# Decode attention with a gated FFN: wo in seven pieces, sixteen partitions of its first piece by way of GpSimd

## The chip, the cores and the metric

The kernel runs on one core of a Trainium2 chip. The metric is the device time of one launch in microseconds, here as the median of several runs. Beside the timed runs there is one execution recorded by the hardware profiler; all times inside the kernel come from that one and count from the start of its span.

## The reference

One token of width 576 goes through a layer norm, and then through two branches whose outputs are added to it: attention of 32 heads over a cache of 16,384 keys and values of width 128, and a feed-forward block with a gelu gate.

```python
xn = _layernorm(x)                                   # (1, 1, 576)
q = (xn @ wq).reshape(B, Sq, 32, 128)                # wq: 576 x 4096
scores = einsum("bhqd,bhkd->bhqk", q, k_cache) * 128 ** -0.5
o = einsum("bhqk,bhkd->bhqd", softmax(scores), v_cache)
A = o.reshape(B, Sq, 4096) @ wo                      # wo: 4096 x 576
g, u = xn @ w_gate, xn @ w_up                        # 576 x 4608 each
Bout = (gelu(g) * u) @ w_down                        # w_down: 4608 x 576
return x + A + Bout
```

Everything is fp32. The two caches are 537 MB, the weights some 50 MB; every byte is read once.

## The kernel before

The program is written in a tile framework that inserts the waits between engines. All large loads are issued by SyncE (SP, the helper `load`, L67 and L68) into three large slots of 64 KB a partition: one of tag "v" (`vslot`) and two of tag "k" (`kslot`). A load may be issued when the slot's last reader is done. First come wq, w_gate and w_up, whose products TensorE makes (`project`, L132). Then the loop over heads (L238) runs: K of head h goes into a kslot; VectorE multiplies it by the query (L204) and sums it over the head's width (L205); TensorE, ScalarE and VectorE make the softmax (L207 to L218); V of the head before goes through TensorE (`pv`, L225). Every fourth head `out_heads` takes the sums out of PSUM (L230 to L235).

Behind the last head stands the part that the change touches. Three tiles are taken: `ta` (a vslot), `tb` (the kslot of the last K) and `te` (the kslot that holds the last V). A matrix of many rows is laid out with several rows to a partition: w_down has 36 of 576 columns on each of the 128 partitions, wo has 32. Such a stretch of 576 columns on all partitions is called a row here; its product takes one column of `hT` or `oT` as the stationary operand. `load_rows` (L276) loads n rows with one transfer:

```python
def load_rows(t, at, src, lo, n):
    load(t[:, at * D : (at + n) * D], src[:, lo * D : (lo + n) * D])
    return [t[:, (at + j) * D : (at + j + 1) * D] for j in range(n)]
```

w_down comes in pieces of 28 rows (into `ta`) and 8 (into `tb`), wo in pieces of 20 (into `tb`, behind w_down's 8) and 6, 3, 2, 1 (into `te`, so not before `pv` of the last head is done). SP issues them in this order. The attention's output is normalised, transposed and written to `oT` by a small transfer from GpSimd (L299); two more from GpSimd (L307) bring x into `x2`.

`add_out` (L267) does the products on TensorE, at L270. For w_down and the first 26 rows of wo a row is split in two halves of 288 columns; even rows go to `acc`, odd ones to `PO[0]`. The last `WO_Q` = 6 rows are split in four quarters of 144 columns, into four partitions of `acc4`. In front of the third row from the end VectorE adds the two half-width sums to x (L314, L315), and TensorE adds the result into the quarters (L318). After the last row VectorE copies `acc4` to SBUF (L322) and SP stores it (L323). Each fp32 matmul appears as two matmul records in the trace.

Of the kernel before, what the change touches and what calls it, by code (L numbers as in the profile page):

```python
# [8 lines left out]
F32 = mybir.dt.float32  # L9
# [4 lines left out]
P = 128  # L14
H, SK, DH = 32, 16384, 128
D, DF = 576, 4608
# [11 lines left out]
WD_T = DF // P  # L28
WO_T = HD // P
WD_PIECES = (28, 8)  # L30
WO_PIECES = (20, 6, 3, 2, 1)
WO_A = 20
WO_Q = 6
QUART = D // 4
HG = 4
PW = 4 * HG
# [4 lines left out]
def kernel(ctx: ExitStack, tc: tile.TileContext, x, k_cache, v_cache, wq, wo, wg, wu, wd, out):  # L41
    nc = tc.nc
    cpool = ctx.enter_context(tc.tile_pool(name="cpool", bufs=1))
# [10 lines left out]
    xf = x.rearrange("b s d -> (b s) d")  # L54
# [3 lines left out]
    wov = wo.rearrange("(p t) f -> p (t f)", t=WO_T)  # L58
# [8 lines left out]
    def load(dst, src):  # L67
        nc.sync.dma_start(dst, src)  # L68
        return dst
# [5 lines left out]
    row3, tails, at = {}, {}, 0  # L75
# [191 lines left out]
    def add_out(groups, lhs, w, last=False):  # L267
        n = D // len(groups)
        for i, g in enumerate(groups):
            nc.tensor.matmul(g, lhs, w[:, i * n : (i + 1) * n], start=id(g) not in seen, stop=last)  # L270
            seen.add(id(g))

    half = [[pairs[i][32 * (2 * i + j) : 32 * (2 * i + j) + 1, :HALF] for j in range(2)] for i in range(2)]
    quart = [acc4[32 * g : 32 * g + 1, :] for g in range(4)]

    def load_rows(t, at, src, lo, n):  # L276
        load(t[:, at * D : (at + n) * D], src[:, lo * D : (lo + n) * D])
        return [t[:, (at + j) * D : (at + j + 1) * D] for j in range(n)]

    ta, tb, te = vslot(), kslot(), kslot()  # L280
    a, b = WD_PIECES
    wd_rows = load_rows(ta, 0, wdv, 0, a) + load_rows(tb, 0, wdv, a, b)
    wo_rows, lo = [], 0
    for n in WO_PIECES:
        wo_rows += load_rows(tb, b + lo, wov, lo, n) if lo < WO_A else load_rows(te, lo - WO_A, wov, lo, n)
        lo += n
# [22 lines left out]
    for j, w in enumerate(wo_rows):  # L309
        if j < WO_T - WO_Q:  # L310
            add_out(half[j % 2], oT[:, j : j + 1], w, last=j >= WO_T - WO_Q - 2)
            continue
        if j == WO_T - 3:
            nc.vector.tensor_add(x2[:64], x2[:64], PO[0][64:, :HALF])  # L314
            nc.vector.tensor_add(x2[:64], x2[:64], acc[:64, :HALF])  # L315
            for i, g in enumerate(quart):
                r, lo = 32 * (i // 2), i % 2 * QUART
                nc.tensor.matmul(g, ones[r : r + 1, :1], x2[r : r + 1, lo : lo + QUART], start=False, stop=False)  # L318
        add_out(quart, oT[:, j : j + 1], w, last=j == WO_T - 1)
# [32 lines left out]
```

## Time and profile before

| | us |
|---|---|
| median of 3 runs | 1372.63 (1372.15 to 1372.82) |
| the profiled execution's own time | 1372.94 |
| its span | 1371.1 |
| VectorE busy | 1128.3 (82% of the span) |
| TensorE busy | 403.5 (29%) |
| ScalarE, GpSimd busy | 38.9, 6.3 |

The page lists busy times, queues, the chain of work that ended last and the costliest groups. In a row of the chain stand start, length and what ran or was waited for; in a row of the timeline the bracket gives the idle time before an instruction and what ended it; in a row of DMA issues the last number is the time from issue to landing. The DMA share of a window is the mean busy share of the core's sixteen DMA engines. PEclk is the clock granted to TensorE, 1.00 being full speed.

### The profile page before, as it was taken

What the parts mean: (1) busy time and instruction counts of PE and PEld (TensorE: products, weight loads), DVE (VectorE), ACT (ScalarE), POOL (GpSimd) and SP (SyncE); (2) the same over time, 40 slices, a digit from 0 to 9 for tenths busy, and PEclk for the clock granted to TensorE, in tenths of its full rate; (3) what the DMA queues carried; (4) which work ended last, traced back from release to release, by engine and by line L of the source; (5) the groups of instructions that cost most, each with busy time, mean ns of one, the idle gap of its engine ahead of it and who ended that gap; (6) DMA issues with size and microseconds to landing.
All of it is one profiled execution on the core that took longest, in us unless ns stands there. A gap on an engine that the chain in (4) does not pass through costs nothing.

```text
span 1371.1 us, 6374 instructions
## 1 busy us (share of the span) xinstructions
PE 403.5 (29%) x2861; PEld 117.2 (9%) x2861; DVE 1128.3 (82%) x160; ACT 38.9 (3%) x128; POOL 6.3 (0%) x17
## 2 busy tenths in 40 slices
PE   4421232322321232322212332322212232322146
PEld 1110000100000000100000000100000000100012
DVE  1059999889888888899888888898888888998830
ACT  0000000000000000000000000000000000000000
POOL 0010000000000000000000000000000000000000
PEclk9775566566556656665556556556556656566577
DMA  9999999999999999999999999999999999999997
GB/s 403 439 428 444 433 428 427 436 434 438 430 430 433 436 435 434 429 432 434 434 433 434 433 434 434 428 434 434 438 432 429 428 436 434 442 427 429 428 427 303
DMA packets 11908, 588.05 MB, mean 429 GB/s; under 512 B 1621, under 2 KB 1641, under 8 KB 2026
## 3 DMA queue, kind: packets, MB, share of 16 engines
q1 hardware_dynamic: 11528, 587.60, 99.2%
q8 instruction: 22, 0.36, 0.1%
q0 software_dynamic: 352, 0.06, 0.0%
q14 instruction: 4, 0.03, 0.0%
q10 hardware_dynamic: 2, 0.00, 0.0%
HBM read 587.60 MB, written 0.00 MB: 429 GB/s over the span
## 4 chain that ended last, share of the span: by engine, by line
DMA 50%; DVE 45%; PE 3%; another core or an unknown queue 1%; issue 1%; ACT 0%; SPq 0%; DVEq 0%
DMA kslot<-in_A_k_cache_dram 45%; DVE kslot L204 23%; DVE s L205 22%; DMA kslot<-in_A_wo_dram 3%; DMA kslot<-in_A_wq_dram 2%; PE pg L132 2%; PE acc L270 1%; PE pt L211 0%; DVE pm L209 0%; PE pq L147 0%; ACT qrow L139 0%; DVE nm L213 0%; DVE kslot L314 0%; DVE kslot L315 0%
## 5 line engine op out<-in xcount | busy, mean ns | idle before, releaser
L204 DVE TENSOR_TENSOR kslot<-kslot,qs 128x16384 f32<-128x16384 f32 (+1 forms) x33 | 551.3, 16706 | 90.6 <-DMA kslot<-in_A_k_cache_dram 90.6
L205 DVE TENSOR_REDUCE s<-kslot 128x128 f32<-128x16384 f32 (+1 forms) x33 | 551.2, 16703 | 3.3
L225 PE MATMUL po<-vslot,pe 128*16 128x512 f32 x1984 | 283.6, 736 | 645.6 <-DMA vslot<-in_A_v_cache_dram 630.2
L225 PEld LDWEIGHTS po<-vslot,pe 128*16 128x16 f32 x1984 | 66.9, 113 | 846.8 <-issue 829.9
L211 PE MATMUL pt<-ident,pm 128*1 128x128 f32 x32 | 11.9, 372 | 237.6 <-DVE pm L209 237.6
L265 DVE MEMSET acc<- 128x144 f32 x1 | 0.2, 178 | 74.3 <-ACT vslot L166 74.3
L132 PE MATMUL pg<-kslot,xnb 128*32 128x384 f32 (+1 forms) x208 | 24.2, 629 | 33.5 <-DMA kslot<-in_B_w_gate_dram 18.4
L314 DVE TENSOR_TENSOR kslot<-kslot,po 64x288 f32<-64x288 f32 x1 | 0.5, 455 | 36.1 <-PE po L270 36.1
L217 ACT ACTIVATE nb<-pb 128x1 f32<-128x1 f32 x32 | 5.5, 171 | 811.8 <-PE pb L215 811.8
L211 PEld LDWEIGHTS pt<-ident,pm 128*1 128x1 f32 x32 | 2.5, 79 | 261.0 <-DVE pm L209 220.2
L215 PE MATMUL pb<-nm,ones 1*128 1x1 f32 x64 | 18.2, 351 | 13.1 <-DVE nm L213 13.1
L213 DVE TENSOR_REDUCE nm<-pt 1x1 f32<-1x128 f32 x32 | 8.9, 278 | 14.9 <-PE pt L211 14.9
L215 PEld LDWEIGHTS pb<-nm,ones 1*128 1x128 f32 x64 | 15.9, 306 | 22.1 <-DVE nm L213 12.0
L147 PE MATMUL pq<-qrow,ones 1*128 1x512 f32 x16 | 15.6, 1072 | 0.0
L270 PE MATMUL acc<-kslot,oT 128*1 128x288 f32 (+1 forms) x100 | 10.8, 410 | 8.2 <-DMA kslot<-in_A_wo_dram 8.2
L218 ACT ACTIVATE pe<-s,nb 128x128 f32<-128x128 f32 x32 | 12.8, 402 | 1.0
L132 PEld LDWEIGHTS pg<-kslot,xnb 128*32 128x32 f32 x208 | 7.2, 129 | 51.4 <-DMA kslot<-in_B_w_gate_dram 19.2
L291 DVE RECIPROCAL rl<-pl 128x32 f32<-128x32 f32 x1 | 0.4, 358 | 13.7 <-PE pl L289 13.7
L270 PE MATMUL acc<-vslot,hT 128*1 128x288 f32 x56 | 8.9, 488 | 7.8 <-DMA vslot<-in_B_w_down_dram 7.8
L230 ACT ACTIVATE o<-po 128x512 f32<-128x512 f32 x8 | 4.8, 597 | 221.8 <-PE po L225 221.8
L234 PE MATMUL pc<-sel,o 128*128 128x4 f32 x64 | 8.4, 255 | 5.7 <-ACT o L230 5.7
L209 DVE TENSOR_REDUCE pm<-s 128x1 f32<-128x128 f32 x32 | 9.2, 286 | 1.1
(74 smaller groups left out, 112.9 us busy)
## 6 DMA issues: line engine op xcount, KB each, us to landing
kslot<-in_A_k_cache_dram SPq DMA_DIRECT2D x2, 4096.0 KB, 27.1
vslot<-in_B_w_down_dram SPq DMA_DIRECT2D x1, 8064.0 KB, 29.0
kslot<-in_B_w_gate_dram SPq DMA_DIRECT2D x1, 6912.0 KB, 55.6
kslot<-in_B_w_up_dram SPq DMA_DIRECT2D x1, 6912.0 KB
kslot<-in_A_wo_dram SPq DMA_DIRECT2D x1, 5760.0 KB, 42.1
vslot<-in_B_w_gate_dram SPq DMA_DIRECT2D x1, 2304.0 KB, 29.0
vslot<-in_B_w_up_dram SPq DMA_DIRECT2D x1, 2304.0 KB, 37.5
kslot<-in_B_w_down_dram SPq DMA_DIRECT2D x1, 2304.0 KB, 28.8
```

The lines of the kernel that those rows point to most:

```text
L132: nc.tensor.matmul(pg[32 * q : 32 * q + 32, b, :size], lhs, rhs[:, lo : lo + size], start=k == 0, stop=k == len(steps) - 1)
L147: nc.tensor.matmul(pq, ones[r : r + 1, :], qrow[r : r + 1, lo : lo + QH * DH], start=True, stop=True)
L204: tc.keep_in_program_order(nc.vector.tensor_mul(blk, blk, Q[h].to_broadcast([P, n, DH])))
L205: nc.vector.tensor_reduce(S[h][:, i : i + n], blk, axis=AX.X, op=ALU.add)
L209: tc.keep_in_program_order(nc.vector.reduce_max(pm, S[h], axis=AX.X))
L211: nc.tensor.transpose(pt[:1, :P], pm, ident)
L213: tc.keep_in_program_order(nc.vector.tensor_reduce(nm, pt[:1, :P], axis=AX.X, op=ALU.max, negate=True))
L215: nc.tensor.matmul(pb[:, :1], ones[:1, :], nm, start=True, stop=True)
L218: nc.scalar.activation(pe4, S.pop(h).rearrange("p (k s) -> p k s", s=4), AF.Exp, bias=nb, scale=SCALE, accum_out=lsum[:, h : h + 1])
L225: nc.tensor.matmul(PO[h // HG % 2][q : q + PW, :], pe[:, lo : lo + PW], vt[:, k * 512 : (k + 1) * 512], start=i == 0 and k < 4, stop=i == ...
L234: nc.tensor.matmul(pc[:, :HG], o4[:, j * DH : (j + 1) * DH], pick[:, j, :], start=j == 0, stop=j == 3)
L270: nc.tensor.matmul(g, lhs, w[:, i * n : (i + 1) * n], start=id(g) not in seen, stop=last)
```

## The change

wo comes in seven pieces, 14, 8, 5, 2, 1, 1, 1, instead of five. The first (14 rows) goes into `tb`, the others into `te`. Quarter width now holds for the last ten rows, and the addition of x stands in front of the fifth row from the end.

The 14 rows are loaded by SP on partitions 0 to 111 alone. Partitions 112 to 119 and 120 to 127 come by one GpSimd transfer each, and in front of each of these stands a tiny GpSimd transfer of eight partitions of 288 B, from x into a tile `junk` that nothing reads. On GpSimd's queue the four stand behind the eight transfers of `gu` at the start of the kernel and ahead of `oT` and the two of x. The first tiny one waits for nothing late; the first eight rows wait for the slot of the last K to be free.

```diff
-WO_PIECES = (20, 6, 3, 2, 1)
-WO_A = 20
-WO_Q = 6
+WO_PIECES = (14, 8, 5, 2, 1, 1, 1)
+WO_A = 14
+WO_Q = 10
+SPLIT = P - 16
...
+    junk = cpool.tile([P, D // 8], F32, name="junk")
+
     def load_rows(t, at, src, lo, n):
-        load(t[:, at * D : (at + n) * D], src[:, lo * D : (lo + n) * D])
+        if src is wov and lo == 0:
+            load(t[:SPLIT, at * D : (at + n) * D], src[:SPLIT, lo * D : (lo + n) * D])
+            for p in range(SPLIT, P, 8):
+                tc.keep_in_program_order(nc.gpsimd.dma_start(junk[p : p + 8, :], xf.rearrange("o (p f) -> (o p) f", p=8)))
+                tc.keep_in_program_order(nc.gpsimd.dma_start(t[p : p + 8, at * D : (at + n) * D], src[p : p + 8, lo * D : (lo + n) * D]))
+        else:
+            load(t[:, at * D : (at + n) * D], src[:, lo * D : (lo + n) * D])
         return [t[:, (at + j) * D : (at + j + 1) * D] for j in range(n)]
...
-        if j == WO_T - 3:
+        if j == WO_T - 5:
```

## The prediction

> **What bounds the kernel now.** I read the page first: its span, its DMA queues and the shares of the chain that ended last.
>
> ```profile
> span 1371.1 us, 6374 instructions
> q1 hardware_dynamic: 11528, 587.60, 99.2%
> q8 instruction: 22, 0.36, 0.1%
> q10 hardware_dynamic: 2, 0.00, 0.0%
> HBM read 587.60 MB, written 0.00 MB: 429 GB/s over the span
> DMA 50%; DVE 45%; PE 3%; another core or an unknown queue 1%; issue 1%; ACT 0%; SPq 0%; DVEq 0%
> ```
>
> The sixteen DMA engines are busy with SP's loads for 99.2% of the span, so the bytes set the length and only the last stretch is open to a change like this one. The second view is the chain in order of time, at its end.
>
> ```profile
> 1314.09 42.11 DMA kslot<-in_A_wo_dram
> 1356.33 0.65 PE acc L270 x2
> 1356.99 0.47 PE acc L270 x2
> ...
> 1364.72 0.24 PE acc L270 x2
> ...
> 1365.52 0.47 DVE kslot L314
> 1366.01 0.46 DVE kslot L315
> 1366.51 0.42 PE acc L318 x8
> 1366.93 0.89 PE acc L270 x24
> 1367.82 0.02 issue
> 1367.85 0.31 DVE kslot L322
> ```
>
> The first piece of wo (twenty rows of 576 columns) lands at 1314.09 + 42.11 = 1356.20. From then on TensorE never waits again: it works through the rows until 1365.5, then come the two adds on VectorE, x, and the last three rows. The third view is the same stretch by windows (TensorE, weight loads, VectorE, ScalarE, GpSimd, then clock, DMA share and GB/s).
>
> ```profile
> 1351.00:1353.00 2.00, 0.00 (x0) 0.00 (x0) 0.00 (x0) 0.00 (x0) 0.00 (x0) 0.62 0.87 371
> 1357.00:1359.00 2.00, 2.00 (x20) 0.59 (x16) 0.00 (x0) 0.00 (x0) 0.00 (x0) 0.50 1.00 411
> 1359.00:1360.00 1.00, 1.00 (x12) 0.30 (x8) 0.00 (x0) 0.00 (x0) 0.00 (x0) 0.50 0.69 279
> 1360.00:1361.00 1.00, 1.00 (x12) 0.30 (x8) 0.00 (x0) 0.00 (x0) 0.00 (x0) 0.50 0.59 242
> 1361.00:1362.00 1.00, 1.00 (x16) 0.39 (x12) 0.00 (x0) 0.00 (x0) 0.00 (x0) 0.65 0.47 191
> 1362.00:1363.00 1.00, 1.00 (x24) 0.38 (x16) 0.00 (x0) 0.00 (x0) 0.00 (x0) 1.00 0.43 164
> 1363.00:1364.00 1.00, 1.00 (x24) 0.38 (x16) 0.00 (x0) 0.00 (x0) 0.00 (x0) 1.00 0.28 111
> 1364.00:1365.00 1.00, 1.00 (x20) 0.38 (x16) 0.00 (x0) 0.00 (x0) 0.00 (x0) 1.00 0.01 2
> ```
>
> Two things are to be seen. The last bytes are in just after 1364, while TensorE ends at 1367.82: behind the last byte stands a backlog of rows, 3.6 us of it, because TensorE was idle until 1356.2 and then ran at half clock until about 1361.7. And the DMA engines do not end together: their share falls from 1.00 to 0.01 over five microseconds. The idle share between 1359 and 1364 is 0.31 + 0.41 + 0.53 + 0.57 + 0.72 = 2.54, so loads spread perfectly would end 2.5 us earlier. Followed packet by packet, about eight engines end by 1361, and the others at 1362.4 to 1364.2; the late ones are those among whose packets the 22 instruction fetches of queue q8 fall, in turn. The one-partition load of x that ScalarE issues (q10) runs on an early one.
>
> **Seven pieces instead of five.** The bytes stay; what changes is how many rows lie behind each landing.
>
> ```profile
> kslot<-in_A_wo_dram SPq DMA_DIRECT2D x1, 5760.0 KB, 42.1
> kslot<-in_A_wo_dram SPq DMA_DIRECT2D x1, 1728.0 KB, 33.9
> kslot<-in_A_wo_dram SPq DMA_DIRECT2D x1, 864.0 KB, 35.6
> kslot<-in_A_wo_dram SPq DMA_DIRECT2D x1, 576.0 KB, 36.6
> 1326.43 1.75 SPq L68 DMA_DIRECT2D kslot<-in_A_wo_dram  x4
> ```
>
> The second piece (six rows) lands at 1326.43 + 33.9 = 1360.3, the third (three rows) at about 1326.9 + 35.6 = 1362.4. That is 4.1 us for six rows and 2.1 for three: 0.7 us a row. The fourth lands at about 1363.9, so the single last row lands at about 1364.55. With pieces of 14, 8, 5, 2, 1, 1, 1 and no other edit the landings are 1356.2 - 6 x 0.69 = 1352.1, then 1357.6, 1361.1, 1362.5, 1363.2, 1363.9, 1364.6.
>
> Now TensorE. The 26 half-width rows take four matmul records each (the chain's steps of two on acc and two on po): 0.48 us a row at half clock, 0.24 at full. A quarter-width row takes eight records: 24 records, three rows, in 0.89 us, so 0.30. Fourteen rows from 1352.1 take 3.4 to 6.7 us, so they end at 1355.5 to 1358.8; the eight of the second piece end at 1359.5 to 1362.6 (the end 1362.6 only if the clock never rises; it rose about 5.4 us after the start at 1356.3, so I take under 1360.5). The five quarter-width rows follow at 1361.1 and end near 1362.7; the two adds on VectorE (0.47 + 0.46) lie beside them; the eight matmuls of x (0.42) come behind, by 1363.1, and the two rows, then one and one, are each done before the next landing. So the backlog is gone and the end hangs on the last landing: 0.13 us to the first matmul (1356.20 to 1356.33, as now), eight matmuls at 0.30 and the run-out of the last one, together 0.45, then the copy at L322: 1364.55 + 0.13 + 0.45 = 1365.15 against 1367.85, which is 2.7 earlier. Each engine now moves its eight partitions in seven stretches instead of five; no row prices that apart, and going by the two completions more I take 0.1 (bounds 0 and 0.3), which leaves 2.6. Four more quarter-width rows are 4 x (0.30 - 0.24) = 0.24 us of TensorE, covered by waits. If TensorE stays at half clock to the very end, rows cost twice and the end comes up to 1.2 us later; I take the full clock, as in the windows from 1362 on, and keep 1.2 for the range.
>
> ```profile
> 1337.25 0.65 PE L270 MATMUL acc<-vslot,hT 128*1 128x288 f32 x2 [7.83 <-DMA vslot<-in_B_w_down_dram]
> ```
>
> The program gives its loads completion counters in turn, and so the last of the seven pieces waits for the load that had its counter before, the first of w_down. TensorE starts on that at 1337.25, so the issue slips to 1337, while 26 us of loads are still queued. Behind it on SP stands only the output's store.
>
> **Sixteen partitions through GpSimd.**
>
> ```profile
> 1330.01 0.56 POOL L299 DMA_DIRECT2D oT<-orow  x1 [1244.59 <-ACT orow L297]
> oT<-orow POOLq DMA_DIRECT2D x1, 16.0 KB, 7.0
> 1317.95 8.42 PE L225 MATMUL po<-kslot,pe 128*16 128x512 f32 x64 [2.57 <-DMA kslot<-in_A_v_cache_dram]
> 1313.72 0.29 DVE L209 TENSOR_REDUCE pm<-s 128x1 f32<-128x128 f32 x1
> ```
>
> GpSimd's queue has nothing between 85 us and 1330, so the first tiny transfer goes out early and the first eight rows wait for the last reduce, which frees the slot at 1313.7. Four issues of 0.56 us end by 1316; oT, the next in the queue, comes at 1330 and is not delayed. GpSimd transfers took 7 us from issue to landing under full load, so the rows lie ready some 25 us before TensorE wants them. They share the engines with V of the last head, on which TensorE waits at 1317.95; a delay of up to 2.4 us there moves pv and SP's next issues, with 25 us of loads queued, and costs nothing.
>
> What counts is which engines carry them. One row of fourteen is 32,256 B; at 429/16 = 26.8 GB/s an engine needs 1.20 us. SP's first piece shrinks from eight partitions an engine to seven: every engine gains 1.20. The sixteen rows go back on: evenly (one each: 0), or both transfers on the same eight (two each: those eight +1.20 net, the others -1.20). No row of the trace shows a transfer of eight partitions, so the bounds on the last landing are -1.2 (all on the early eight: late ones end at 1363.35, early ones by 1361 + 1.2 = 1362.2, still ahead) and +1.2 (on late ones, or on a mixed eight). The nearest row, q10's one-partition load on an early engine, says that a transfer too narrow for sixteen engines starts on early ones; I take -1.2.
>
> [...]
>
> **The sum.** 2.6 + 1.2 = 3.8 us off the profiled execution's 1372.94 (span 1371.1 and 1.84 around it): 1369.1. The median is 0.3 lower, 1372.63, so the forecast is 1368.8. About 0.2%, 2.75 us, is what a measurement of this kernel tells from no change; 3.8 is above it.
>
> **Rivals.**
> Even or wrong half: pieces gain 2.6, placement 0 or -1.2 (a loss): 1370.0 or 1371.2. For it: nothing in the rows fixes the engines. Against: q10's row. Chance 0.22, nearly all within 0.2%.
>
> Narrow writes collide (slower). In every load of before, an engine writes its own eight partitions and no other engine does. If the way into such a group is no wider than one engine's 26.8 GB/s, the moved rows queue: eight rows on eight engines squeeze into one or a few groups that their usual engine is filling too. A row then takes between 1.2 us (nothing shared) and 9.6 (eight in one group); I take a value in between: with half the eight in a group, with its usual engine beside them, make 5 x 1.2 = 6.0. Two rows are 12.0, less the 1.2 that the engine gave up: +10.8. The early engines have 3.1 us in hand (1361 to 1364.2), so the last landing is 7.7 later: 1370.0 + 7.7 = 1377.7. It decides for slower than before from 2.6 us of delay on. The load of 112 partitions, seven an engine, would also straddle groups and could add as much again. For it: the rate per engine never goes over 27 GB/s in the windows, even when half of them are idle (111 GB/s at a share of 0.28 is 25 an engine). Against: that holds as well if the engine itself is the limit; every load of before is full width, so no row tells. Chance 0.33.
> [...]
>
> The tiny transfers or the rows do not go as written (all of a transfer on one engine: 8 x 1.2 = 9.6 us on it per transfer): 0.05, at 1376 to 1386.
>
> **How the numbers follow.** Forecast 0.40 at 1368.8, its own range 1368.2 to 1370.0 (cold TensorE); even or wrong half 0.22; collision 0.33, of which 0.05 is mild enough to stay within 0.2%; astray 0.05. Faster: 0.40 + 0.04 = 0.44; within 0.2%: 0.18 + 0.05 = 0.23; slower: 0.28 + 0.05 = 0.33. The range from 1368.2 to 1378.0 leaves out the upper third of the collision case (0.12), the astray case (0.05) and a little below: under 0.2.
>
> **What would show it.** Right: first wo landing near 1351, TensorE idle in front of each of the last rows with wo as releaser, the L322 copy at 1364.0, DMA share staying above 0.6 until 1362. Backlog claim wrong: TensorE without waits from the first landing to the end. Collision: GpSimd's wo rows landing well over 10 us after issue, the 112-partition piece later than 1352, a DMA tail longer than the five microseconds of now.

## The result, and the profile after

The changed kernel takes 1394.61 us (median of four runs, 1393.89 to 1396.36), the kernel before 1372.72 beside it (1372.15 to 1373.36): ratio 1.0164, 95% interval 1.0152 to 1.0176. It is 22 us slower. The forecast of 1368.8 had the wrong sign, and the time lies far above the range, whose upper end was 1378.0. The profiled execution took 1394.79, with a span of 1393.0.

The chain of work that ended last, at its end (start, length, what ran or was waited for):

```profile
1385.00 0.14 issue
1385.13 2.14 PE acc L271 x40
1387.28 0.58 PE acc L327 x8
1387.86 1.98 PE acc L271 x40
1389.84 0.02 issue
1389.86 0.31 DVE kslot L331
```

The copy of the result (now L331) starts at 1389.86, against 1367.85 before. TensorE's own row says where those 22.0 us arose. The timeline of TensorE, four rows from the last head on; the bracket is its idle time and what ended it:

```profile
1317.49 8.67 PE L226 MATMUL po<-kslot,pe 128*16 128x512 f32 x64 [2.57 <-DMA kslot<-in_A_v_cache_dram]
...
1348.38 0.65 PE L271 MATMUL acc<-vslot,hT 128*1 128x288 f32 x2 [19.17 <-DMA vslot<-in_B_w_down_dram]
1359.14 0.41 PE L271 MATMUL acc<-kslot,hT 128*1 128x288 f32 x2 [2.27 <-DMA kslot<-in_B_w_down_dram]
1375.61 0.64 PE L271 MATMUL acc<-kslot,oT 128*1 128x288 f32 x2 [14.35 <-DMA kslot<-in_A_wo_dram]
```

V of the last head is as punctual as before. The first product with w_down, whose loading the change does not touch, starts 11.1 us later (1337.25 before), and the first with wo starts at 1375.61 (1356.33 before), after 14.35 us of waiting. So there are two delays, one inside the loading of w_down and one inside wo. The DMA issues, with KB each and the time from issue to landing in the last column, first one of before and then those of now:

```profile
vslot<-in_B_w_down_dram SPq DMA_DIRECT2D x1, 8064.0 KB, 29.0
```

```profile
vslot<-in_B_w_down_dram SPq DMA_DIRECT2D x1, 8064.0 KB, 40.3
kslot<-in_A_wo_dram SPq DMA_DIRECT2D x1, 3528.0 KB, 61.9
...
kslot<-in_A_wo_dram POOLq DMA_DIRECT2D x2, 252.0 KB, 24.4
...
oT<-orow POOLq DMA_DIRECT2D x1, 16.0 KB, 18.6
```

GpSimd's rows need 24.4 us instead of the 7 that the prediction took, and everything that is queued with them is late: w_down's first piece 40.3 (29.0 before), `oT` 18.6 (7.0 before). Windows of four microseconds, whose last two numbers are the share of the sixteen DMA engines that is busy and what they move. A row counts whole, with all its bytes and all its time, in the window in which it starts, so long rows make one window too full and the next too empty:

```profile
1314.00:1318.00 4.00, 1.10 (x6) 0.68 (x10) 0.28 (x1) 0.67 (x3) 1.28 (x3) 0.50 1.67 428
1318.00:1322.00 4.00, 4.00 (x28) 0.94 (x24) 0.00 (x0) 0.00 (x0) 0.00 (x0) 0.65 0.47 73
1354.00:1358.00 4.00, 2.87 (x48) 0.94 (x40) 0.00 (x0) 0.00 (x0) 0.00 (x0) 1.00 1.00 215
1362.00:1366.00 4.00, 0.00 (x0) 0.00 (x0) 0.00 (x0) 0.00 (x0) 0.00 (x0) 0.89 0.93 204
1374.00:1378.00 4.00, 2.39 (x24) 0.75 (x28) 0.00 (x0) 0.00 (x0) 0.00 (x0) 0.50 0.93 362
```

The third and fourth are the sight to remember: all engines busy (1.00, 0.93), and half the bytes (215 and 204 GB/s instead of some 430). That is the loading of 112 partitions. The first two belong to GpSimd's rows, and there the counting by starts shows: a share of 1.67 is followed by one of 0.47. With every row spread over the time that it took, all sixteen engines are busy from 1318 to 1322 and move 155 GB/s. The records of single transfers' rows say the same. A row of 32,256 B took 1.94 to 4.88 us by way of GpSimd (median 3.78) and 2.40 by way of SP's 112 partitions (median), and w_down's rows of 64,512 B up to 7.37 us, where before their median was 2.38.

### The profile page after: what moved, and what is told of

Same layout as the page of the kernel before. It is cut to its first block, busy times and chain, and to the rows that moved or that the text cites. A ratio compares the mean times of both kernels' runs of the same rounds, so it can differ in the third digit from the quotient of the medians.

```text
span 1393.0 us, 6417 instructions
## 1 busy us (share of the span) xinstructions
PE 406.4 (29%) x2877; PEld 118.0 (8%) x2877; DVE 1128.3 (81%) x160; ACT 38.9 (3%) x128; POOL 8.4 (1%) x21
## 4 chain that ended last, share of the span: by engine, by line
DMA 49%; DVE 44%; PE 3%; another core or an unknown queue 2%; issue 1%; ACT 0%; DVEq 0%; SPq 0%
DMA kslot<-in_A_k_cache_dram 44%; DVE kslot L205 22%; DVE s L206 22%; DMA kslot<-in_B_w_down_dram 3%; DMA kslot<-in_A_wq_dram 2%; PE pg L133 2%; PE acc L271 1%; PE pt L212 0%; PE pq L148 0%; ACT qrow L140 0%; DVE pm L210 0%; DVE nm L214 0%; PE acc L327 0%; SPq L69 0%
## 5 line engine op out<-in xcount | busy, mean ns | idle before, releaser
L133 PE MATMUL pg<-kslot,xnb 128*32 128x384 f32 (+1 forms) x208 | 24.5, 636 | 32.8 <-DMA kslot<-in_B_w_gate_dram 18.0
L271 PE MATMUL acc<-kslot,oT 128*1 128x144 f32 (+1 forms) x124 | 11.4, 415 | 16.6 <-DMA kslot<-in_A_wo_dram 16.5
## 6 DMA issues: line engine op xcount, KB each, us to landing
vslot<-in_B_w_down_dram SPq DMA_DIRECT2D x1, 8064.0 KB, 40.3
```

Source lines behind the costliest of these rows:

```text
L133: nc.tensor.matmul(pg[32 * q : 32 * q + 32, b, :size], lhs, rhs[:, lo : lo + size], start=k == 0, stop=k == len(steps) - 1)
```

## The experiments

Theory (shared ways), a hypothesis of the author's: an engine writes into SBUF through a way that belongs to a set of partitions and is no wider than the engine; in a load of 128 partitions each engine would have one to itself, and rows that another engine writes into the same set would slow both. No trace names the engine of a row, so the runs can show only what should follow from this. Rival (GpSimd's path): transfers of eight partitions, or ones with GpSimd's issue, are slow by themselves, and the rest is queueing.

**The pieces alone.** Against before:

```diff
-WO_PIECES = (20, 6, 3, 2, 1)
-WO_A = 20
-WO_Q = 6
+WO_PIECES = (14, 8, 5, 2, 1, 1, 1)
+WO_A = 14
+WO_Q = 10
...
-        if j == WO_T - 3:
+        if j == WO_T - 5:
```

> Seven pieces, all on 128 partitions from SP; no GpSimd rows, no tiny transfers. The backlog theory (TensorE's rows behind the last byte are what the pieces take away): 2.6 us faster than before, 1370.0 to 1370.2; TensorE waits for wo before the last rows, and the L322 copy starts some 0.6 us behind the last landing. Rival (smaller pieces cost as much as they free): within 0.5 us of before, or slower.

Measured 1370.13 (before 1372.41 beside it), ratio 0.9984, interval 0.9975 to 0.9993. TensorE's waits in this kernel:

```profile
1352.09 0.64 PE L270 MATMUL acc<-kslot,oT 128*1 128x288 f32 x2 [4.74 <-DMA kslot<-in_A_wo_dram]
1361.07 1.41 PE L270 MATMUL acc<-kslot,oT 128*1 128x144 f32 x40 [1.01 <-DMA kslot<-in_A_wo_dram]
1363.84 0.43 PE L270 MATMUL acc<-kslot,oT 128*1 128x144 f32 x8 [0.16 <-DMA kslot<-in_A_wo_dram]
1364.55 0.43 PE L270 MATMUL acc<-kslot,oT 128*1 128x144 f32 x8 [0.29 <-DMA kslot<-in_A_wo_dram]
```

The end of the chain, and one window while the first piece comes:

```profile
1307.55 29.31 DMA vslot<-in_B_w_down_dram
...
1336.88 27.63 DMA kslot<-in_A_wo_dram
...
1365.04 0.31 DVE kslot L322
```

```profile
1346.00:1350.00 4.00, 1.35 (x24) 0.34 (x16) 0.00 (x0) 0.00 (x0) 0.00 (x0) 1.00 0.98 418
```

TensorE waits for the load ahead of the last rows: the backlog is gone and the end hangs on the last landing. This half of the change is a gain, and the loss lies wholly in the other half: 24.5 us between this run and the changed kernel.

**112 partitions without GpSimd's rows.** Against the changed kernel; what GpSimd would bring is left out, and those partitions hold zeros:

```diff
+            nc.vector.memset(t[96:, at * D : (at + n) * D], 0.0)
             load(t[:SPLIT, at * D : (at + n) * D], src[:SPLIT, lo * D : (lo + n) * D])
-            for p in range(SPLIT, P, 8):
-                ...
```

> As the changed kernel, but nothing comes by GpSimd: partitions 112 to 127 of the first fourteen rows are left out (set to zero by VectorE). Theory of shared ways (a group of partitions takes in no more than one engine's 27 GB/s, and seven partitions an engine straddle the groups): the 112-partition load still runs at half rate, its rows of 32,256 B at 2.4 us as in the changed kernel, and the end is 6 to 10 us behind that of the pieces alone, about 1377 to 1380. Rival (only GpSimd's transfers hurt): its rows take 1.20 us, and the kernel is at or 1 us below the pieces alone, about 1369 to 1370.

Measured 1381.79, ratio 1.0069 (1.0055 to 1.0082): 11.7 over the pieces alone, though an eighth fewer bytes are moved in this piece. The chain's end, and one window while the piece comes:

```profile
1336.47 39.75 DMA kslot<-in_A_wo_dram
1376.22 0.04 issue
1376.27 0.47 PE acc L271 x8
1376.74 0.02 issue
1376.76 0.31 DVE kslot L327
```

```profile
1354.00:1358.00 4.00, 0.00 (x0) 0.00 (x0) 0.00 (x0) 0.00 (x0) 0.00 (x0) 0.50 1.09 231
```

The wait for the last piece is 39.75 us; with the pieces alone it was 27.63. The engines are busy all the time and move 231 GB/s, where the same piece on 128 partitions moved 418; the rows' median is 2.39 us, twice 1.20. No GpSimd transfer of wo is in this kernel, so the rival can't explain it. Setting the zeros holds VectorE for 6.8 us and the loads behind them back with it, but w_down's loading runs on meanwhile and is in at the old time (1336.5), so that this is not the cause. An estimate by the theory: shared evenly over sixteen engines, 128 partitions are eight each and 112 are seven, so that an engine's seven would no longer fall into one set of eight.

**Narrow transfers without the 112.** The pieces alone, and beside them six extra rows of sixteen partitions into a place that nothing reads, by two GpSimd transfers with tiny ones ahead of them:

```diff
+EXTRA = 6
...
+    junk = cpool.tile([P, D // 8], F32, name="junk")
...
+        if src is wov and lo == 0:
+            ex = slice((at + n) * D, (at + n + EXTRA) * D)
+            for i, ps in enumerate((slice(112, 120), slice(120, 128))):
+                ... dma_start(junk[8 * i : 8 * i + 8, :], ...)
+                ... dma_start(t[ps, ex], src[ps, : EXTRA * D])
```

> Seven full-width pieces from SP, and beside them the two GpSimd transfers with their tiny ones, of six more rows (13,824 B a partition) into unused columns of the same tile, on partitions 112 to 119 and 120 to 127; what they bring isn't read. [...] If the GpSimd part is harmless: about 0.5 us, the price of 221 KB more.

**The same bytes on spread partitions.** One line differs:

```diff
-            for i, ps in enumerate((slice(112, 120), slice(120, 128))):
+            for i, ps in enumerate((slice(0, 32, 4), slice(1, 32, 4))):
```

> The same bytes by the same two GpSimd transfers and tiny ones as in the narrow run, but on partitions 0, 4, ..., 28 and 1, 5, ..., 29, each of the eight four partitions from the next. [...] Rival (GpSimd's way of sending): as the narrow run, to 1 us.

Measured 1374.39 (1.0014, 1.0005 to 1.0023) and 1370.86 (0.9987, 0.9978 to 0.9997). One link of the chain in the first and in the second, the landing of w_down's first piece:

```profile
1307.41 34.15 DMA vslot<-in_B_w_down_dram
```

```profile
1307.91 29.13 DMA vslot<-in_B_w_down_dram
```

With the pieces alone this link is 29.31. In the first the rows of 13,824 B took 0.52 to 1.49 us, and w_down's up to 4.34; in the second all sixteen took 0.52 or 0.53, as SP's rows of this size did before (median 0.52), and w_down's row stayed at 2.38. Issue, tiny transfers and bytes are equal; only the partitions differ, and with them the rows of wo that are read. So the rival falls: the same bytes by the same path cost 4.3 us over the pieces alone on 112 to 127 and 0.7 on the spread partitions. That the first write where another engine writes is the theory's reading of it.

**Two transfers of 64 partitions.** Against the pieces alone:

```diff
-        load(t[:, ...], src[:, ...])
+        if src is wov and lo == 0:
+            for p in (0, 64):
+                load(t[p : p + 64, ...], src[p : p + 64, ...])
+        else:
+            load(t[:, ...], src[:, ...])
```

> The seven pieces, everything loaded by SP, but the first piece (14 rows) in two transfers of 64 partitions each, 0 to 63 and 64 to 127. All sixteen engines then write 64 partitions at a time, so two engines stand on each group of eight partitions. Shared ways: a row of 32,256 B takes 2.4 us instead of 1.20 as in the run with 112 partitions, the piece runs at about half of 429 GB/s, and its 4.1 MB take some 9.6 us longer: 1378 to 1381 (the run with the pieces alone: 1370.1). Rival, that only a count of partitions that is no multiple of sixteen is slow (112 gives seven partitions an engine): rows of 1.20 us and 1369.8 to 1371.

Measured 1385.24, ratio 1.0091 (1.0076 to 1.0106): 15.1 over the pieces alone, more than expected. A window while the piece comes:

```profile
1354.00:1358.00 4.00, 0.00 (x0) 0.00 (x0) 0.00 (x0) 0.00 (x0) 0.00 (x0) 0.50 0.91 196
```

Half rate (196 GB/s) with a count that divides by sixteen, so 112 is not slow for being odd. By the theory what counts is whether each engine has its own partitions; the run shows the half rate, not which engine wrote where. The 5 us that were not expected are rows of the pieces before and behind it (18,432 B, up to 1.91 us instead of 0.69). They are slow while rows of the two transfers run beside them (1337 to 1366 us), as the theory would have it if engines that are done with one load are already in the next.

**Without the tiny transfers**, in the changed kernel and in the one with spread partitions:

```diff
-    junk = cpool.tile([P, D // 8], F32, name="junk")
...
-                ... dma_start(junk[...], xf.rearrange("o (p f) -> (o p) f", p=8))
```

> The changed kernel without the two tiny transfers. Shared ways: the sixteen long rows write the same sixteen partitions, whoever carries them, and SP's 112-partition load stays: 1392 to 1397 (changed kernel 1394.6). Rival, that the tiny ones decide (by setting which engines carry the rows, or by standing ahead of them): over 3 us away from the changed kernel, on either side; without them both long transfers may fall on different sets of eight engines, one row for each engine instead of two for eight of them.

> The run with the extra six rows of sixteen partitions spread over 0 to 31, without the two tiny transfers. [...] If the tiny ones do not decide which engines carry the rows, all sixteen rows take 0.52 us again and the time is that with the tiny ones, 1370.9.

Measured 1396.78 (1.0173, 1.0156 to 1.0190) and 1370.16 (0.9984, 0.9975 to 0.9993). The first is 2.2 us above the changed kernel (summed as in the table below, its rows lose 27.0 us against 23.9), the second 0.7 below its twin. That 0.7 says nothing of the tiny ones: the ten runs of either kernel lie near 1370.1 or near 1370.9, three and seven with the tiny transfers, six and four without, and the median falls to the larger group. In the second, fifteen of the sixteen rows took 0.52 or 0.53 us, and seven of the second transfer's eight start 5.28 us behind one of the first's, which speaks for the same eight engines under both transfers, without the tiny ones too. The tiny transfers are not what decides here: beside a loss of 24.5 they spare some 2 us at most (four runs each, whose times overlap), and by what way isn't settled.

**Where all of it went.** The time of every row of the last loads can be summed in the trace and compared with the pieces alone. Divided by sixteen engines, the surplus is the time lost, as far as it falls evenly on them:

| surplus over the pieces alone, us of row time | w_down 64,512 B | wo 32,256 B | 18,432 B | others | sum / 16 | measured |
|---|---|---|---|---|---|---|
| changed kernel | 126.5 | 170.3 | 83.7 | 1.2 | 23.9 | 24.5 |
| 112 partitions alone | 0 | 114.8 | 67.6 | 0 | 11.4 | 11.7 |
| six narrow rows, 112 to 127 | 53.4 | 0 | 0 | 13.7 | 4.2 | 4.3 |
| the same, spread | 0 | 0 | 0 | 8.3 | 0.5 | 0.7 |
| two of 64 partitions | 0 | 156.6 | 76.4 | 0 | 14.6 | 15.1 |

The sums are those of the profiled executions, the last column goes by medians; the profiled executions themselves lie 24.8, 11.7, 4.4, 0.1 and 14.9 above the pieces alone. In the fourth row the surplus is the extra bytes alone, and the profiled execution shows next to nothing of it. An estimate of how the first row is made up: the 4.3 of six narrow rows, taken for fourteen, give 10.0, and with the 11.7 of 112 partitions alone 21.7 of the 24.5. In the first row of the table, GpSimd's sixteen rows make 58.2 of the 32,256 B column and SP's 112 rows 266.0, as in the second (268.7).

**Can the imbalance between the engines be used?** With the pieces alone eight of the sixteen engines finish the last piece 3.3 to 5.0 us behind the first one, the others by 2.1 us. The spread run, whose profiled execution ends 0.1 us later for all its extra bytes on partitions 0 to 31, led to the author's guess that the early eight write partitions 0 to 63; no run shows which engine writes which partition. On that guess, and by the theory, whole ways have to be relieved: thirty rows on all partitions, and the last two of all 128 source partitions on partitions 0 to 63, by eight GpSimd transfers. A second small transfer brings the part of the attention's output that belongs to them.

```diff
-WO_PIECES = (14, 8, 5, 2, 1, 1, 1)
+WO_PIECES = (14, 8, 4, 2, 1, 1)
+LOW = 2
...
+    low = tb[:64, (b + WO_A) * D : (b + WO_A + 2 * LOW) * D]
+    wlow = wov[:, WO_M * D :].rearrange("(a q) f -> q a f", a=2)
+    for c in [s + r for s in (0, 32) for r in range(4)]:
+        ... dma_start(low[c : c // 32 * 32 + 32 : 4, :]..., wlow[c : c // 32 * 32 + 32 : 4])
...
```

> [...] In the run with the pieces alone the sixteen parts of the last landing come 0 to 2.1 us (eight early engines) and 3.3 to 5.0 us (eight late ones) behind the first. If the early eight are those of partitions 0 to 63, each early one moves 1.37 us more (two rows of eight partitions at 26.8 GB/s) and each late one 1.37 less: the last landing comes 1.4 us earlier, 1368.7 (pieces alone 1370.1). If early and late engines are not the two halves of the partitions, the worst late one still gains or loses up to 1.4: 1370 to 1371.5.

Measured 1372.77 (1.0007, 0.9997 to 1.0016): no gain, and 2.8 over the pieces alone. The attention's output was late behind the eight transfers:

```profile
kslot<-in_A_wo_dram POOLq DMA_DIRECT2D x8, 72.0 KB, 25.5
...
oT<-orow POOLq DMA_DIRECT2D x1, 16.0 KB, 25.1
```

SP's rows of 32,256 B had a median of 1.31 us instead of 1.20. Each transfer held two stretches a partition, sixteen in all. The first transfer's stretches start in two groups of eight, the second group 2.55 us behind the first one by one, which speaks for eight engines with two each and against sixteen at once; all took 0.18 us. By their starts the second transfer's stand behind rows of the other eight engines; they took up to 0.26, and w_down's rows beside them rose from 2.38 to as much as 2.69. So it looks as if at least the first two transfers went to one half of the engines and then to the other: the late eight would not be relieved, and by the theory would write into the others' ways besides. The next edit makes sixteen transfers of eight stretches, the second eight behind x:

```diff
+    def load_low(a):
+        for c in [s + r for s in (0, 32) for r in range(4)]:
+            ps = slice(c, c // 32 * 32 + 32, 4)
+            ... dma_start(low[ps, a * LOW * D : (a + 1) * LOW * D], wlow[ps, a])
...
```

> [...] Now sixteen transfers of eight stretches; the second eight are issued behind the attention's output and x, and their products stand in front of the last two rows. If eight stretches go to the eight early engines, as in the run with the spread partitions, the rows take 0.18 us each and SP's 32,256 B rows 1.20, each early engine carries 1.37 us more and each late one 1.37 less: 1368.7. If GpSimd's rows, one behind each of SP's on an engine, come too late for TensorE (eight transfers of two steps behind SP's rows of 0.7 to 2.4 us take some 15 to 40 us), it is 1370 to 1375, with a wait of TensorE on GpSimd's rows or on the attention's output.

Measured 1371.47 (0.9995, 0.9986 to 1.0004). Most of SP's rows were back at 1.20 (up to 1.31). Fourteen of the sixteen parts of the last landing had come by 1363.4, which is 1.1 earlier than the 1364.5 at which the pieces alone are in; the last two came at 1364.3 and 1365.7. TensorE waited for the four-row piece, whose last part was late as well, and then worked without a wait to 1366.20, 0.5 us behind the last landing:

```profile
1362.85 1.16 PE L272 MATMUL acc<-kslot,oT 128*1 128x144 f32 x32 [2.20 <-DMA kslot<-in_A_wo_dram]
```

So moving these rows brings most of the landing forward nearly as worked out (1.1 of 1.4), and two stragglers take it back. Why they straggle wasn't settled. One thing more is to be had from this run. In the experiments before, the rows of wo that are read change together with the partitions that are written, so a slow source would look the same as a slow destination. The second eight transfers here read rows that belong to partitions 64 to 127 and write them on 0 to 63, and all but one of their stretches took 0.18 us. That speaks for the destination; a run that moves the source alone was not made.

**The pieces alone once more**, on the chip of the first of these two:

> The seven pieces alone once more, on the same chip as the run before it, so that the two can be compared: 1369.8 to 1370.4.

Measured 1370.01, ratio 0.9985 (0.9976 to 0.9993), against 1372.77 for the first attempt. The seven pieces with full-width loads by SP are the fastest version measured: it beats the kernel before and the changed one.

## Why the prediction was wrong

**The pieces: right, in mechanism and about in size.** The step said 2.6 us off the end; the run measured 2.3 by the medians, and 2.81 in the trace (copy at 1365.04 against 1367.85). (Its sum 1364.55 + 0.13 + 0.45 is 1365.13, not 1365.15; nothing hangs on it.) First landing of wo worked out at 1352.1, TensorE's first wo row at 1352.09; the short waits ahead of the last rows came as written. TensorE was at full clock at the end (1.00 in the windows from 1358 to 1366), so the 1.2 us kept for half clock were not needed.

**The placement: the step that failed.** With the cover, which comes next, it was to save 1.2 us and cost 24.5. The prediction took -1.2 us, from "every engine gains 1.20" for a piece of seven partitions an engine, and two rows back on the early eight. Both prices are a row of 32,256 B at 1.20 us. The runs show that number only in loads of all 128 partitions. In the changed kernel SP's rows took about 2.40 each: at seven an engine (an estimate, 112 over sixteen) 16.8 us where eight had taken 9.6. That is 7.2 lost, and with the loads around it, which suffer too, it is 11.4 by the table (112 partitions alone) and 11.7 measured. Its guess that the rows go to the early eight engines may be right: the spread rows, sent the same way, ran undisturbed at 0.52 us on partitions 0 to 31, and in the profiled execution left the last landing where it was (0.1 us later), as they would on the early eight. For the changed kernel itself no run shows which engines carried them. The guess rested on one narrow load of another queue, so it would be luck, and it was of no use: six rows by the same two transfers cost 4.3 us on 112 to 127 and 0.7 on the spread partitions.

**The cover: wrong.** The rows were to land 7 us after issue and "lie ready some 25 us before TensorE wants them", sharing engines at no cost beyond V. They took 24.4, and w_down, queued with them, came 11 us late. Not all of the 24.4 is collision. The spread run's rows, none of them slow, took this long from issue to landing:

```profile
kslot<-in_A_wo_dram POOLq DMA_DIRECT2D x2, 108.0 KB, 14.7
```

There a GpSimd row starts as a row of SP's ends (one at 1320.02), and SP's rows are 2.38 us long; with eight of the sixteen rows on the engines by 1320.8, the other eight came 10 us later. So the 7 us of a single small transfer was no price for four in a row, whatever they write. The delay was not bounded by V's slack of 2.4 us because it did not end with V.

**The collision rival: right in kind, a chance of 0.33, and too small.** It gave the last landing 7.7 us more than the pieces alone have (1377.7); it came 24.1 later (1364.5 and 1388.6). Its price for one GpSimd row, 6.0 us, was too high (3.8). What its sum left out was the other side of the collision: it charged the eight engines that carry the rows, and not the rows of the loads beside them. In the table w_down's rows lose 126.5 us, more than twice what GpSimd's rows took altogether (58.2). The load of 112 partitions, put at "as much again" and left out of the sum, is half the loss (11.7 of 24.5). Slow rows are what the traces show; that shared ways make them slow stays the author's theory. The three signs named for it (rows landing well over 10 us after issue, the 112-partition piece later than 1352, a longer tail of loads) are all in the trace, but the first would not have told: 14.7 us without a collision. The argument against it, that no row of before tells, was no argument: in before every large load was full width, so the case of the change was outside what the trace could price, and a bound from the rows of full-width loads is not a bound.

The other rivals did not decide: even or wrong half is worth 1.2 or 2.4 us beside a loss of 24.5, and the tiny transfers neither saved nor sank it (2.2 us at most).

## What to carry to other kernels

A row's duration in a trace is a price for the pattern of partitions that it was measured in: here a load of all 128 partitions ran its rows at 1.20 us, and one of 112 or 64 at 2.4, half the rate with all engines busy. A narrow transfer beside a stream slowed the stream's rows too: six rows on 112 to 127 cost w_down's rows 53.4 us, spread over 0 to 31 none. When a change cuts a partition range or adds such a transfer, charge both the new rows and the rows of the stream; surplus row time over sixteen engines gave the loss here to within 0.6 us. Smaller last pieces are worth having by themselves: test the parts of a combined change apart.

## What was not expected of the hardware

A load of 112 of 128 partitions moved 204 to 231 GB/s in the windows shown, with all engines busy, where one of 128 moved 418: an eighth fewer bytes, and rows of 2.39 us instead of 1.20. Sixteen rows of 32,256 B in sixteen neighbouring partitions, half a megabyte, brought the whole stream down to 155 GB/s for four microseconds, with all sixteen engines busy. Sixteen rows of 13,824 B in steps of four partitions cost nothing beyond their bytes (0.52 us each).
